# Retention and feed-forward in one kernel: the second chunk's recurrence in halves of 64 tokens, its scores and state sums issued apart

## The chip, the cores and the metric

The kernel runs on one core of a Trainium2 chip. A core has five engines that run side by side, each through its own list of instructions: TensorE (PE in the profile, with its weight loads as PEld), VectorE (DVE), ScalarE (ACT), GpSimd (POOL) and SyncE (SP, which here issues the transfers). They wait for each other by semaphores. The metric is the time of the whole program on the device, in microseconds, from repeated runs. All arithmetic is in fp32.

## The reference

Two layers follow each other. The first is a retention layer: for every batch (4) and head (8) a state of 64x64 is carried over 768 tokens. The second is a feed-forward layer of width 2048 with a leaky ReLU on 3072 rows of 512.

```
for t in range(S):                       # S = 768, D = 64
    state = gamma * state + outer(k[t], v[t])
    y[t]  = scale * (q[t] @ state)
x = y, heads side by side                # 3072 x 512
h = x @ w_in                             # 512 x 2048
out = max(0.01 * h, h) @ w_out           # 2048 x 512
```

`gamma` differs by head. Over a block of tokens the recurrence is the same as three products: the scores `k q`, masked to earlier tokens and multiplied with the block's values; a read of the state as it stood before the block; and the block's sum of `k v`, which is added to the state. The decay is put into `v` beforehand and into the result afterwards.

## The kernel before, in words

The tokens go in six chunks of 128 (`C`), each with all four batches. For each chunk the recurrence makes the layer's input `x`, and the feed-forward layer is worked in four units `u` of 512 hidden columns: `hidden` makes `g`, `output` makes `o` from it. Both use a scheme of seven products instead of eight, M1 to M7 (`seven`, product on line 662), which needs differences of blocks of `x` and `g` (`differences`, lines 606 and 609) and sums of weight blocks (`add_sums`, `last_sum`). The very first unit of chunk 0 is done plainly, in four steps for each half of the batches (`direct`, line 683).

The weights arrive as 64-bit words in pieces. ScalarE makes each piece's powers (`next_powers`, lines 578 to 583) and VectorE its mantissas (`next_mantissas`, lines 590, 595 and 602). A piece's raw words have three places, so the load of a later piece starts when VectorE has read an earlier one.

The order of the work is written out by hand: the engines execute the statements in the order in which the program issues them. Around the change this is the list of statements from line 957 on. In the names, `(1, b)` is chunk 1, batch `b`.

Before the change chunks 0 and 1 do the recurrence over all 128 tokens of a chunk at once. `score` (line 191) makes the scores of one batch, `masked` (line 211) multiplies with the mask on VectorE, `reads` (line 226) reads the state, `last_values` (261) and `first_values` (250) multiply scores and values, `state` (276) makes the sum for the state, `tokens_taken` (306) brings the result into `x`, and `state_taken` (312) adds the sum to the state. A pair of batches is done together by `products_together`. Batch 1's scores use two single banks of the dense products' pool (`score_apart`).

Chunks 2 to 5 use another form, by halves of 64 tokens and by pairs of batches. `scores_of_pair` makes scores (line 369) and both halves' state sums (line 380), masks (387), and makes the state at the middle and at the end of the chunk by two additions. `joint_visit` then multiplies the values (444), reads the state of each half (427) and takes the results (466), batch 1 before batch 0. In chunk 2 this goes into PSUM tiles of two banks, tag `att`, of which there are two places that are given out in turn: scores, sums, first and second results.

`JOINED` says from which chunk on the inputs are laid out for the second form: `q` and `k` per batch as before, but keys of a pair together and values of a pair together.

Of the kernel before, what the change touches and what calls it, by code (L numbers as in the profile page):

```python
# [22 lines left out]
def kernel(  # L23
# [113 lines left out]

    def early_inputs(c, b, kind, k):
        def do():
            place = place_of_unit(k, f"in{c}{b}_{kind}")  # L140
            flat = place.rearrange("p i k n -> p (i k n)")
            half = 2 * HP * C
            heads[c, b + kind] = [flat[:, 0:half].rearrange("p (s a t) -> p s a t", s=2, a=HP)]
            load_qk(c, b + kind)
            of_pair(c, b, kind, flat[:, half : 2 * half].rearrange(
                "p (n h d) -> p n h d", n=2, h=H))
            rooms[kind] = flat[:, 2 * half : 2 * half + 2 * HP * D]
        return do

    def spare(kind):  # L150
        return lambda: rooms[kind].rearrange("p (n a d) -> p n a d", n=2, a=HP)
# [68 lines left out]
    def reads(c, b):  # L220
        x = heads[c, b][0]
        if (c, b) not in sums_at:
            sums_at[c, b] = apart(two_banks(f"yp_{c}_{b}"))
        ps = sums_at[c, b]
        for j, m, i, a in pairs:
            mm = nc.tensor.matmul(ps[j][ts(i, 64), m, :], lhsT=st[b][ts(j, 64), a, :],
                                  rhs=x[ts(j, 64), 0, a, :], start=(m == 0), stop=False,
                                  skip_group_check=True)

        reads_done[c, b] = nc.gpsimd.memset(between, 0.0).ins  # L230
        tc.add_manual_dep(reads_done[c, b], mm.ins.name, IN_ORDER, reason="rows of the array")

    reads_done = {}
# [9 lines left out]
    def first_values(c, b):  # L243

        y, am, ps = heads[c, b][1], scores[c, b], sums_at[c, b]
        for m in range(HP // 2):
            for i in range(2):
                for j in range(2):
                    s, a = i ^ j, 2 * m + i
                    mm = nc.tensor.matmul(ps[j][ts(i, 64), m, 0:64],  # L250
                                          lhsT=y[ts(s, 64), 1, 2 * a + j, :],
                                          rhs=am[ts(s, 64), j, m, 0], start=False, stop=True,
                                          skip_group_check=True)
                    if (c, b) in reads_done:
                        tc.add_manual_dep(mm.ins, reads_done.pop((c, b)).name, IN_ORDER,
                                          reason="rows of the array")
# [73 lines left out]
    def score_apart(c, b):  # L330

        banks = [ffs.tile([128, HP * C], FP32, tag="ff", bufs=4, name=f"ap{j}_{c}_{b}")[:, 0:NS]
                 for j in range(2)]
        scores[c, b] = [ps.rearrange("p (m n t) -> p m n t", n=3, t=C // 2) for ps in banks]
        scores_to(heads[c, b][0], scores[c, b])

    def masked_apart(c, b, j):
        if j == 0:
            weights_of[c, b] = new_am(c, b)
        nc.vector.tensor_tensor(  # L340
            out=weights_of[c, b][:, j].rearrange("p m n t -> p m (n t)"),
            in0=scores[c, b][j].rearrange("p m n t -> p m (n t)"),
            in1=mask.rearrange("p n t -> p (n t)").unsqueeze(1)
                .to_broadcast([128, HP // 2, 3 * C // 2]), op=ALU.mult)
        if j == 1:
            scores[c, b] = weights_of.pop((c, b))

    weights_of = {}

# [6 lines left out]
    def scores_of_pair(c, b, banks=None, mid=None):  # L356

        if b == 0 and c > JOINED:
            next_gq()
        banks = banks or bank  # L360
        at = [banks[j].rearrange("p (b m i t) -> p b m i t", b=2, m=HP // 2, i=2)
              for j in range(2)]
        sums = [banks[2 + h].rearrange("p (b a d) -> p b a d", b=2, a=HP) for h in range(2)]
        for n in range(2):
            x = heads[c, b + n][0]
            for m, i, a in quads:
                for h in range(2):
                    for j in range(2):
                        nc.tensor.matmul(at[j][ts(h, 64), n, m, i],  # L369
                                         lhsT=x[ts(j, 64), 1, a, ts(h, 64)],  # L370
                                         rhs=x[ts(j, 64), 0, a, ts(h, 64)],
                                         start=(n == 0 and a == 0), stop=True,
                                         skip_group_check=True)
        last = c == NC - 1
        for n in range(2):
            key, val = keys.pop((c, b + n)), vals[c, b + n]
            for a in range(HP):
                for j in range(2):
                    for h in range(1 if last else 2):
                        nc.tensor.matmul(sums[h][ts(j, 64), n, a], lhsT=key[ts(h, 64), 2 * a + j],  # L380
                                         rhs=val[ts(h, 64), 2 * a + j],
                                         start=(n == 0 and a == 0), stop=True,
                                         skip_group_check=True)
        weights = scores[c, b] = []
        for j in range(2):
            am = work.tile([128, 2, HP // 2, 2, C // 2], FP32, tag=f"am{j}", name=f"am{j}_{c}_{b}")
            nc.vector.tensor_tensor(
                out=am.rearrange("p b m i t -> p (b m i) t"),
                in0=at[j].rearrange("p b m i t -> p (b m i) t"),
                in1=mask[:, 0].unsqueeze(1).to_broadcast([128, 2 * HP, C // 2]), op=ALU.mult)  # L390
            weights.append(am)
# [11 lines left out]
        if following(c, b) is not None and c > JOINED:  # L403
            of_pair(*following(c, b), 0)
# [7 lines left out]
    def joint_visit(c, b, banks=None):  # L412

        later = following(c, b) if c > JOINED else None
# [66 lines left out]
    def early_scores(c, b, place):  # L481
        def do():
            banks = [pair_of_banks(f"{name}_{c}_{b}") for name in ("ap", "sp")]
            scores_of_pair(c, b, banks[0] + banks[1], place())
        return do

    def early_visit(c, b):
        def do():
            joint_visit(c, b, [pair_of_banks(f"yp{n}_{c}_{b}") for n in range(2)])
        return do  # L490
# [366 lines left out]
    load(1, 0, unit_tile(LATE[2], "in10"))  # L857
    load(1, 1, unit_tile(LATE[1], "in11"))
# [60 lines left out]
    load(1, 2, unit_tile(LATE[0], "in12"))  # L919
# [15 lines left out]
    load(1, 3)  # L935
# [8 lines left out]
    def scored_later(b):  # L944
        score(1, b)
        masked(1, b)

    def products_together(b):
        for i in range(2):
            reads(1, b + i)  # L950
        for i in range(2):
            last_values(1, b + i)
            state(1, b + i)
        for i in range(2):
            first_values(1, b + i)

# [5 lines left out]
    scored_later(0)  # L962
    decay_v(1, 1, nc.scalar)
    next(steps)
    score_apart(1, 1)
    next_powers()
    next_mantissas()
    for j in range(2):
        masked_apart(1, 1, j)
    next_powers()  # L970
    products_together(0)
    next_mantissas()
    decay_v(1, 2, nc.scalar)
# [60 lines left out]
    def place_of_unit(k, name):  # L1034
        return work.tile([128, 7, 2, 256], FP32, tag=f"late{k}", name=name)
# [36 lines left out]
    def next_heads():  # L1072
# [15 lines left out]
        (1, 3): dict(s0=[begin_x(2), early_scores(2, 2, spare(1))],  # L1088
# [10 lines left out]
        (0, 3): dict(s0=[begin_units, early_scores(2, 0, spare(0))],  # L1099
# [159 lines left out]
    scores_of_pair(3, 0)  # L1259
# [17 lines left out]
    for n in range(N2):  # L1277
# [22 lines left out]
        if c + 1 < NC and u < 2 and following(c + 1, 2 * u):  # L1300
            scores_of_pair(*following(c + 1, 2 * u))
# [20 lines left out]
JOINED = 2  # L1322
# [87 lines left out]
```

## Time and profile before

| what | value |
|---|---|
| median of 3 runs | 638.65 us (638.64 to 639.24) |
| span of the profiled run | 637.2 us |
| TensorE busy | 630.4 us |
| VectorE busy | 462.3 us |
| ScalarE busy | 269.0 us |
| first small product of chunk 1 on TensorE | at 27.58 us |
| dense step after chunk 1's last product | at 44.63 us |
| granted TensorE clock | 1.000 |

The page gives for each engine the time in which it was busy and its share of the span. A timeline line gives the start in microseconds, the length from the first start to the last end, the engine, the line of the kernel, the tile written and those read, the shape and the count (on TensorE an fp32 product counts as two instructions). What stands in brackets at its end is idle time before it and what ended it. Lengths of neighbours overlap, because instructions are pipelined; the distance from start to start is what a group costs. In a line of busy time by stretches come: the stretch, its length, then busy time and count of PE, PEld, DVE, ACT and POOL, the granted clock, the share of the DMA engines and GB/s.

### The profile page before, as it was taken

How to read it: one execution, taken by the hardware profiler on the slowest of the kernel's cores; microseconds unless marked ns; L12 is line 12 of the kernel's file. 1: busy time of each engine (PE TensorE's matmuls, PEld its weight loads, DVE VectorE, ACT ScalarE, POOL GpSimd, SP SyncE). 2: the span in 40 equal slices, each digit the busy share in tenths (PEclk: the TensorE clock that was granted, in tenths of full speed). 3: DMA queues.
4: the chain of work that ended last, by engine and by line, in shares of the span. 5: the costliest groups of instructions: out<-in, count | busy, mean ns of one | idle time of the engine just before them, and what ended most of it. 6: DMA issues, size and time to landing. Idle time of an engine off the chain costs nothing.

```text
span 637.2 us, 14289 instructions
## 1 busy us (share of the span) xinstructions
PE 630.4 (99%) x6086; PEld 569.1 (89%) x6086; DVE 462.3 (73%) x760; ACT 269.0 (42%) x515; POOL 22.6 (4%) x45
## 2 busy tenths in 40 slices
PE   8999999999999999999999999999999999999997
PEld 5888888888888889899999999999999999999996
DVE  5679769889979976576786666877737768636655
ACT  5876556347343124242352342424333423534421
POOL 2000000000011010101000101000010000000000
PEclk9999999999999999999999999999999999999999
DMA  8931426455863999366735392864455336454301
GB/s 334 405 125 38 127 67 227 141 181 188 287 245 119 341 307 306 103 236 198 253 87 192 111 298 79 268 195 136 137 175 178 89 123 195 153 164 156 87 0 67
DMA packets 87536, 113.42 MB, mean 178 GB/s; under 512 B 3240, under 2 KB 71720, under 8 KB 87472
## 3 DMA queue, kind: packets, MB, share of 16 engines
q1 hardware_dynamic: 87168, 111.88, 53.1%
q8 instruction: 48, 0.79, 0.5%
q10 hardware_dynamic: 304, 0.62, 0.3%
q14 instruction: 16, 0.13, 0.1%
HBM read 93.35 MB, written 19.14 MB: 177 GB/s over the span
## 4 chain that ended last, share of the span: by engine, by line
PE 95%; DVE 2%; ACT 1%; DMA 1%; issue 0%; DVEq 0%; ACTq 0%
PE bank L662 32%; PE bank L1181 27%; PE C_h L662 4%; PE B_o L662 4%; PE A_h L662 4%; PE C_o L662 4%; PE A_o L662 4%; PE B_h L662 4%; PE D_h L662 2%; PE D_o L662 2%; PE d L683 2%; PE bank L369 1%; PE bank L444 1%; PE bank L427 1%; PE bank L380 1%; DMA t<-decay_dram 1%
## 5 line engine op out<-in xcount | busy, mean ns | idle before, releaser
L606 DVE TENSOR_TENSOR made<-made,bank 128x512 f32<-128x512 f32 (+1 forms) x96 | 56.3, 618 | 57.0 <-PE bank L1181 52.8
L606 DVE TENSOR_TENSOR o<-o,bank 128x512 f32<-128x512 f32 (+2 forms) x91 | 58.6, 662 | 53.4 <-PE bank L662 32.8
L662 PE MATMUL bank<-g,w 128*128 128x256 f32 x384 | 89.9, 382 | 0.0
L662 PEld LDWEIGHTS bank<-g,w 128*128 128x128 f32 x384 | 70.7, 190 | 9.2
L1181 PEld LDWEIGHTS bank<-x,wb 128*128 128x128 f32 x672 | 77.6, 192 | 0.8
L1181 PE MATMUL bank<-x,wb 128*128 128x128 f32 x672 | 77.6, 275 | 0.0
L1181 PE MATMUL bank<-x,wa 128*128 128x128 f32 x512 | 68.7, 276 | 0.1
L662 PE MATMUL bank<-gd,w 128*128 128x256 f32 x288 | 66.1, 379 | 0.0
L1181 PEld LDWEIGHTS bank<-x,wa 128*128 128x128 f32 x512 | 63.8, 192 | 1.9 <-ACT bank L1185 0.8
L662 PEld LDWEIGHTS bank<-gd,w 128*128 128x128 f32 x288 | 54.7, 190 | 7.4
L1181 PE MATMUL bank<-t,wa 128*128 128x128 f32 x384 | 53.3, 275 | 0.0
L1223 ACT ACTIVATE g<-g 128x512 f32<-128x512 f32 x64 | 39.3, 631 | 30.8 <-DVE g L606 30.8
L1181 PEld LDWEIGHTS bank<-t,wa 128*128 128x128 f32 x384 | 48.0, 192 | 0.0
L1185 ACT COPY bank<-bank 128x512 f32<-128x512 f32 (+1 forms) x32 | 16.7, 522 | 67.8 <-PE bank L1181 67.5
L606 DVE TENSOR_TENSOR g<-made 128x512 f32<-128x512 f32 x64 | 42.7, 689 | 1.2
L755 ACT COPY bank<-bank 128x512 f32<-128x512 f32 x17 | 9.7, 570 | 71.2 <-PE bank L662 71.1
L609 DVE TENSOR_TENSOR gd<-g,gd 128x512 f32<-128x512 f32 x48 | 33.2, 692 | 5.4 <-ACT g L1223 0.5
L773 ACT COPY bank<-bank 128x512 f32<-128x512 f32 x16 | 9.1, 570 | 46.4 <-PE bank L662 46.4
L662 PE MATMUL bank<-g,last 128*128 128x256 f32 x120 | 28.3, 380 | 0.0
L662 PE MATMUL bank<-gd,last 128*128 128x256 f32 (+1 forms) x124 | 27.5, 373 | 0.0
L662 PE MATMUL A_h<-x,w 128*128 128x256 f32 x112 | 26.6, 380 | 0.0
L662 PEld LDWEIGHTS bank<-gd,last 128*128 128x128 f32 x124 | 22.8, 190 | 3.2 <-DVE gd L609 0.3
(223 smaller groups left out, 1028.2 us busy)
## 6 DMA issues: line engine op xcount, KB each, us to landing
wa<-kept SPq DMA_DIRECT2D x16, 1344.0 KB, 7.2
raw<-in_weights_dram SPq DMA_DIRECT2D x31, 512.0 KB, 4.4
wb<-kept SPq DMA_DIRECT2D x16, 896.0 KB, 5.7
wa<-kept SPq DMA_DIRECT2D x16, 448.0 KB, 4.5
wb<-kept SPq DMA_DIRECT2D x16, 448.0 KB, 6.3
out_dram<-o SPq DMA_DIRECT2D x23, 256.0 KB, 2.9
kept<-w SPq DMA_DIRECT2D x12, 448.0 KB, 5.9
qk<-in_qk_dram SPq DMA_DIRECT2D x10, 512.0 KB, 8.5
```

Source lines behind the costliest of these rows:

```text
L369: nc.tensor.matmul(at[j][ts(h, 64), n, m, i], lhsT=x[ts(j, 64), 1, a, ts(h, 64)], rhs=x[ts(j, 64), 0, a, ts(h, 64)], start=(n == 0 and a = ...
L380: nc.tensor.matmul(sums[h][ts(j, 64), n, a], lhsT=key[ts(h, 64), 2 * a + j], rhs=val[ts(h, 64), 2 * a + j], start=(n == 0 and a == 0), sto ...
L427: mm = nc.tensor.matmul(at[n][j][ts(i, 64), m, ts(h, 64)], lhsT=by_half[h][ts(j, 64), n, a], rhs=x[ts(j, 64), 0, a, ts(h, 64)], start=(n = ...
L606: nc.vector.tensor_tensor(out=out, in0=a, in1=b, op=ALU.add)
L609: nc.vector.tensor_tensor(out=out, in0=a, in1=b, op=ALU.subtract)
L662: nc.tensor.matmul(to, lhsT=block(w, sa)[:, k, ts(i, 128)], rhs=rhs[:, k, a:z], start=(first and (i == 0 or split) and n == 0 and k == 0), ...
L683: nc.tensor.matmul(banks[r][:, i, :], lhsT=block(2 * u, r + 2 * kh)[:, k, ts(i, 128)], rhs=x[:, 2 * kh + th, k, :], start=(step == 0 and i ...
L755: nc.scalar.copy(out=bank_of("B"), in_=ps)
L773: nc.scalar.copy(out=bank_of("D"), in_=ps)
L1181: nc.tensor.matmul(ps[q][:, i], lhsT=w[:, j, i], rhs=part_of(moving[i], s), start=(i == 0 and m in ("M1", "M5", "M4")), stop=True, skip_gr ...
L1185: nc.scalar.copy(out=ps[3], in_=ps[0])
L1223: nc.scalar.activation(g[:, i], g[:, i], AF.Prelu, alpha=0.01)
```

## The change

Chunk 1 goes over to the form of chunks 2 to 5: pairs of batches, halves of 64 tokens. It is meant to take work from TensorE, and to need fewer small groups. In it the two parts of `scores_of_pair` are separated by a `yield`: scores and masks first, state sums and additions in a second step, with one dense step of the feed-forward layer between them. For the later chunks both steps still run one after the other. `early_visit` asks for the tile of the pair's second batch first. The inputs of chunk 1 are loaded by pairs (`inputs_into`). The functions that only the old form used go away (`reads`, `score_apart`, `masked_apart`, `scored_later`, `products_together`).

The core of the diff:

```diff
 def scores_of_pair(c, b, banks=None, mid=None):
...
+        weights = scores[c, b] = []
+        for j in range(2):
+            am = work.tile([128, 2, HP // 2, 2, C // 2], FP32, tag=f"am{j}", name=f"am{j}_{c}_{b}")
+            nc.vector.tensor_tensor(
...
+            weights.append(am)
+        yield
         last = c == NC - 1
         for n in range(2):
             key, val = keys.pop((c, b + n)), vals[c, b + n]
...
-        weights = scores[c, b] = []
-        for j in range(2):
...
-    def early_scores(c, b, place):
+    def early_scores(c, b, place, apart=False):
         def do():
             banks = [pair_of_banks(f"{name}_{c}_{b}") for name in ("ap", "sp")]
-            scores_of_pair(c, b, banks[0] + banks[1], place())
+            steps = scores_of_pair(c, b, banks[0] + banks[1], place())
+            next(steps)
+            if apart:
+                return steps
+            next(steps, None)
         return do
 
     def early_visit(c, b):
         def do():
-            joint_visit(c, b, [pair_of_banks(f"yp{n}_{c}_{b}") for n in range(2)])
+            banks = [pair_of_banks(f"yp{n}_{c}_{b}") for n in (1, 0)]
+            joint_visit(c, b, banks[::-1])
         return do
...
-    load(1, 0, unit_tile(LATE[2], "in10"))
-    load(1, 1, unit_tile(LATE[1], "in11"))
+    inputs_into(unit_tile(LATE[2], "in11"), 1, 0, 1)
+    inputs_into(unit_tile(LATE[1], "in10"), 1, 0, 0)
...
     steps = direct(0, 0, x, parts[0][1], 1)
     next(steps)
-    scored_later(0)
     decay_v(1, 1, nc.scalar)
+    sums_apart = early_scores(1, 0, spare(1, 0, 0), apart=True)()
+    next_powers()
     next(steps)
-    score_apart(1, 1)
-    next_powers()
-    next_mantissas()
-    for j in range(2):
-        masked_apart(1, 1, j)
-    next_powers()
-    products_together(0)
+    next(sums_apart, None)
+    next(steps)
+    early_visit(1, 0)()
     next_mantissas()
     decay_v(1, 2, nc.scalar)
+    decay_v(1, 3, nc.scalar)
     next_powers()
-    decay_v(1, 3, nc.scalar)
-    taken(1, 0, x1)
-    taken(1, 1, x1)
-    next(steps)
-    scored_later(2)
-    scored_later(3)
+    sums_apart = early_scores(1, 2, spare(1, 2, 1), apart=True)()
+    next_mantissas()
     later = hidden(1, 0, x1, t1, *parts[1][1:], order=FIRST)
     next(later)
     last_sum(0)
+    next_powers()
+    next(sums_apart, None)
+    early_visit(1, 2)()
     next_mantissas()
-    products_together(2)
     next_powers()
     run(steps, {})
-    tokens_taken(1, 2, x1)
-    tokens_taken(1, 3, x1)
     differences(x1, t1)
     next_gq()
-    state_taken(1, 2, for_state(sums_at[1, 2]))
-    state_taken(1, 3, for_state(sums_at[1, 3]))
     run(later, {0: [next_mantissas], 1: [lambda: differences(*parts[0][1:])],
                 2: [next_powers], 3: [lambda: add_sums(1)]})
...
-JOINED = 2
+JOINED = 1
```

More of the change, by code (lines that the diff above doesn't have):

```diff
@@ L136, in of_pair, with inputs_into, spare @@
         nc.sync.dma_start(out=place, in_=kv[c, b + kind])
+    def inputs_into(place, c, b, kind):
+        flat = place.rearrange("p i k n -> p (i k n)")
+        half = 2 * HP * C
+        heads[c, b + kind] = [flat[:, 0:half].rearrange("p (s a t) -> p s a t", s=2, a=HP)]
+        load_qk(c, b + kind)
+        of_pair(c, b, kind, flat[:, half : 2 * half].rearrange("p (n h d) -> p n h d", n=2, h=H))
+        rooms[c, b, kind] = flat[:, 2 * half : 2 * half + 2 * HP * D]
     def early_inputs(c, b, kind, k):
         def do():
[L140 to L147, printed above, removed]
-        return do
-    def spare(kind):
-        return lambda: rooms[kind].rearrange("p (n a d) -> p n a d", n=2, a=HP)
+            inputs_into(place_of_unit(k, f"in{c}{b}_{kind}"), c, b, kind)
+        return do
+    def spare(c, b, kind):
+        return lambda: rooms[c, b, kind].rearrange("p (n a d) -> p n a d", n=2, a=HP)
     def load(c, b, place=None):
@@ L218 @@
     pairs = [(j, m, i, 2 * m + i) for m in range(HP // 2) for j in range(2) for i in range(2)]
[L220 to L233, printed above, removed]
     IN_ORDER = mybir.DependencyInfo(mybir.DependencyClass.Sync, mybir.DependencyReason.DATA)
@@ L249, in first_values @@
                     s, a = i ^ j, 2 * m + i
[L250 to L256, printed above, removed]
+                    nc.tensor.matmul(ps[j][ts(i, 64), m, 0:64],
+                                     lhsT=y[ts(s, 64), 1, 2 * a + j, :],
+                                     rhs=am[ts(s, 64), j, m, 0], start=False, stop=True,
+                                     skip_group_check=True)
     def last_values(c, b):
@@ L328 @@
     room = {}
[L330 to L348, printed above, removed]
     halves_of_states = [const.tile([128, 2, HP, D], FP32, name="more_states")]
@@ L356, in scores_of_pair @@
     def scores_of_pair(c, b, banks=None, mid=None):
-        if b == 0 and c > JOINED:
+        if b == 0 and c > 2:
             next_gq()
@@ L373, in scores_of_pair @@
                                          skip_group_check=True)
+        weights = scores[c, b] = []
+        for j in range(2):
+            am = work.tile([128, 2, HP // 2, 2, C // 2], FP32, tag=f"am{j}", name=f"am{j}_{c}_{b}")
+            nc.vector.tensor_tensor(
+                out=am.rearrange("p b m i t -> p (b m i) t"),
+                in0=at[j].rearrange("p b m i t -> p (b m i) t"),
+                in1=mask[:, 0].unsqueeze(1).to_broadcast([128, 2 * HP, C // 2]), op=ALU.mult)
+            weights.append(am)
+        yield
         last = c == NC - 1
@@ L383, in scores_of_pair @@
                                          skip_group_check=True)
-        weights = scores[c, b] = []
-        for j in range(2):
[L386 to L391, printed above, removed]
         p = b // 2
@@ L402, in scores_of_pair @@
         mid_of[p] = old, mid
-        if following(c, b) is not None and c > JOINED:
+        if following(c, b) is not None and c > 2:
             of_pair(*following(c, b), 0)
@@ L412, in joint_visit @@
     def joint_visit(c, b, banks=None):
-        later = following(c, b) if c > JOINED else None
+        later = following(c, b) if c > 2 else None
         banks = banks or [[bank[k] for k in at] for at in ((1, 2), (0, 7))]
@@ L918 @@
     decay_v(0, 2, nc.scalar)
-    load(1, 2, unit_tile(LATE[0], "in12"))
+    inputs_into(unit_tile(LATE[0], "in13"), 1, 2, 1)
     masked(0, 2)
@@ L934 @@
     next_mantissas()
-    load(1, 3)
+    heads[1, 2] = [work.tile([128, 2, HP, C], FP32, tag="qk", bufs=AHEAD, name="qk_1_2")]
+    load_qk(1, 2)
+    of_pair(1, 2, 0)
     values(0, 3)
@@ L942 @@
     add_sums(0, last=False)
[L944 to L955, printed above, removed]
     xs[1] = new_x(1)
@@ L1087 @@
                      s5=[sum_of_unit(3, 0)], s6=[sum_of_unit(3, 1), early_decays(2, 2)]),
-        (1, 3): dict(s0=[begin_x(2), early_scores(2, 2, spare(1))],
+        (1, 3): dict(s0=[begin_x(2), early_scores(2, 2, spare(2, 2, 1))],
                      s1=[sum_of_unit(3, 2)], s2=[sum_of_unit(3, 3)],
@@ L1098 @@
         (1, 2): dict(s0=[sum_of_unit(2, 3)], s1=[keep_unit(2)]),
-        (0, 3): dict(s0=[begin_units, early_scores(2, 0, spare(0))],
+        (0, 3): dict(s0=[begin_units, early_scores(2, 0, spare(2, 2, 0))],
                      s1=[lambda: differences(*parts[1][1:])],
@@ L1258 @@
     halves_of_states.append(work.tile([128, 2, HP, D], FP32, tag="m5", name="half_states"))
-    scores_of_pair(3, 0)
+    products(scores_of_pair(3, 0), 2)
     for b in range(2):
@@ L1300 @@
         if c + 1 < NC and u < 2 and following(c + 1, 2 * u):
-            scores_of_pair(*following(c + 1, 2 * u))
+            products(scores_of_pair(*following(c + 1, 2 * u)), 2)
         if visiting:
```

## The prediction

> **What bounds the kernel now.** I read the page from the top: shares first, then the chain that ended last.
>
> ```profile
> span 637.2 us, 14289 instructions
> PE 630.4 (99%) x6086; PEld 569.1 (89%) x6086; DVE 462.3 (73%) x760; ACT 269.0 (42%) x515; POOL 22.6 (4%) x45
> PE 95%; DVE 2%; ACT 1%; DMA 1%; issue 0%; DVEq 0%; ACTq 0%
> ```
>
> TensorE (PE) is busy 99% of the span and is 95% of the chain. So a microsecond taken off PE in any stage is a microsecond off the end, and a microsecond for which PE waits is one added. The question is only what happens between the first small product of chunk 1 and the return to dense work. That stage is 27.58 to 44.63 us; by stretches (time, PE, weight loads, VectorE, ScalarE, ...):
>
> ```profile
> 27.50:44.60 17.10, 16.82 (x410) 14.17 (x409) 11.91 (x21) 13.84 (x38) 0.39 (x4) 1.00 0.59 215
> 44.60:56.80 12.20, 12.20 (x64) 10.75 (x57) 11.75 (x20) 6.40 (x13) 0.00 (x0) 1.00 0.17 51
> ```
>
> The reader is to see two things. PE has almost no hole in the stage, although VectorE (DVE) works for 11.91 of 17.10 us there. And in the next 12.2 us VectorE is busy 11.75: it has no room to catch up. Work pushed out of the first stretch arrives late in the second.
>
> How PE spends the stage now, from the timeline (start, length, engine, line, what, count):
>
> ```profile
> 27.58 0.90 PE L191 MATMUL ap<-in 64*64 64x128 f32 x32
> 28.41 1.99 PE L683 MATMUL d<-x,w 128*128 128x256 f32 x8
> 30.33 0.90 PE L191 MATMUL ap<-in 64*64 64x128 f32 x32
> ...
> 35.40 1.99 PE L683 MATMUL d<-x,w 128*128 128x256 f32 x8
> 37.32 0.90 PE L191 MATMUL ap<-in 64*64 64x128 f32 x32
> ...
> 38.82 1.99 PE L662 MATMUL A_h<-x,w 128*128 128x256 f32 x8
> 40.65 0.38 PE L695 MATMUL B_h<-mask 128*128 128x512 bf16 x1
> ...
> 44.63 1.99 PE L683 MATMUL d<-x,w 128*128 128x256 f32 x8
> ```
>
> Each pair of batches has a dense group between its scores and its products: VectorE's masks run behind it. At 35.40 a dense group also stands between the first pair's products and the second pair's scores; VectorE takes the first pair's results (from 35.52) behind that one.
>
> What the new form costs can be read off chunk 2, which already uses it:
>
> ```profile
> 191.88 1.16 PE L369 MATMUL ap<-in 64*64 64x64 f32 x64
> 192.86 1.11 PE L380 MATMUL sp<-in,in 64*64 64x64 f32 x64
> 193.90 1.99 PE L662 MATMUL C_h<-t,w 128*128 128x256 f32 x8
> 201.01 0.46 PE L444 MATMUL yp<-am,in 64*64 64x64 f32 x16
> 203.17 1.99 PE L662 MATMUL C_h<-x,w 128*128 128x256 f32 x8
> ```
>
> Scores and sums take 2.02 us together, a visit 2.16 us. But there 7.1 us of dense work lie between sums and visit.
>
> [...] VectorE's instructions start in program order throughout. [...] A dense group with small tiles on both sides takes 1.92 us here (28.41 to 30.33) against 1.73 us among dense ones, so I use the former. [...] the masks of 128x512 take 0.68 us each here[...].
>
> **The change, part by part.** PE, from the unchanged 27.58 us, start to start:
>
> - scores of pair 0: 1.04 (the small group before a dense one, as 192.86 to 193.90), to 28.62;
> - dense group 1.92, to 30.54; sums 1.04, to 31.58; dense group 1.92, to 33.50;
> - visit 2.10 (2.16 less the switch, since small tiles follow), to 35.60;
> - scores of pair 1: 1.04; group M1 into A_h 1.83 (38.82 to 40.65); fill 0.31 (40.65 to 40.96); sums 0.98; visit 2.16, to 41.92.
>
> Without waits the dense group of 44.63 would begin at 41.92: 2.71 us saved. This is the part the change removes: whole-token value products, wider reads, and about 0.8 us of small waits.
>
> Data is no limit. The decayed values of batch 1 are ready at 29.62 (ScalarE, unchanged), before sums at 30.54. The first pair's inputs come by the same four transfers in the same order; only which half lies in each differs. ScalarE then decays batches 2 and 3 in one run: 29.62, 1.9 for one piece's powers, 4.0 for 16 decays, to 35.5; sums of pair 1 come after that.
>
> Now the waits it adds, which the line order decides. Banks alternate between two places. In the new order, VectorE's queue after the first visit is: four takes, a weight piece's mantissas (three operations), two masks, another piece's mantissas, `last_sum`, the two additions of state sums, four takes, a third piece, then the differences.
>
> First wait: the scores of pair 1 go into the banks from which batch 1's results are taken, and no dense group lies between. In the visit batch 1 is complete about 2.07 us after its start (203.00 plus 0.07 from the end of its last product to a VectorE start, as 44.47 to 44.54), so takes begin at 35.57. Two takes are done 0.75 us later. PE waits from 35.60 to 36.37: 0.77 us. If one bank sufficed it would be 0.4.
>
> Second wait: `read(0)` of the second visit writes the banks that hold the state sums, so it waits for both additions. VectorE from 35.57: takes 1.33 (its cadence at 207.66 to 208.99), mantissas 1.9 (33.66 to 35.52), masks 1.20 (195.26 to 196.46), mantissas 1.9, `last_sum` 0.60 (40.04 to 40.64), additions 1.40 (196.46 to the end of the second at 197.86). The sum is 8.33, to 43.90, and PE goes on at 44.00. PE itself, with the first wait, is at `read(0)` at 36.37+1.04+1.83+0.31+0.98+0.28 = 40.81. It waits 3.19 us. Queued behind it on PE is everything, the dense group that needs nothing from VectorE included. If only the first addition were needed, the wait would be 2.5. The masks, done at 40.0, cost nothing: M1, fill and sums hide them.
>
> The remaining 1.88 us of the visit end at 45.88: the dense group is 1.25 us later than before.
>
> Third wait: C_h needs the first difference. Before, the differences came at once after the takes. Now a piece's mantissas stand between. Takes from 45.79, 1.33, mantissas 1.9, a difference 0.69: 49.71. PE would start C_h at 45.88+1.84+1.72 = 49.44. 0.3 us lost.
>
> Fourth: VectorE is then about 2.5 us later than before (the 0.7 us of separate state additions at 48.52 is gone, the 1.9 is added), PE 1.6 us. The copy into B_o at 58.88 has 0.8 us to spare before PE's 60.28, and it stands behind three ScalarE operations that wait for VectorE. 0 to 0.4 us; I take 0.2. After 61 us VectorE idles (2.16 us at 74.42), and the delay is absorbed.
>
> Everything later is the same work in the same order, with the state buffers' names changed. The earlier mask instruction in the text of the other chunks changes no engine's order. Sum: -2.71+0.77+3.19+0.31+0.2 = +1.76 us: 640.4.
>
> **Rivals.**
>
> - *The waits just eat the saving.* If banks free earlier (one take, one addition), first and second waits shrink by 0.4 and 0.7, and the last two vanish: 638.65-2.71+0.4+2.5+0.1 = about 638.9. For it: the estimates of readiness are to a tenth. Against it: both places are allotted as two-bank tiles.
> - *The saving comes through.* If VectorE's queue were not the limit: 638.65-2.71+0.8 = 636.7. For it: VectorE has 5 us idle in the stage now, and chunk 2 shows no such wait. Against it: the queue adds up to 8.3 us where PE has 5.2 us of work, and its idle time falls before 35.5, where it cannot be used.
> - *The delay spreads.* The pieces' raw loads start as their mantissas end, 5 to 6 us later than now. If the converted weights then miss the first output groups, another 1 to 2 us: about 642. Against it: page and stretch show under a fifth of the DMA engines busy from 44.6 to 56.8.
>
> **How the numbers follow.** Forecast 0.60, waits eating the saving 0.22, saving through 0.11, spreading 0.07. A change of 0.2% is 1.28 us, so slower begins at 639.93. Some 0.07 of the forecast falls under that. Slower 0.53+0.07 = 0.60; same 0.22+0.07 = 0.29; faster 0.11. The range reaches from the second case, 638.6, to between forecast and spreading, 641.6.
>
> **What would show it.** Right: PE idle ahead of the reads of the second visit (from about 40.8 to 44.0), released by VectorE's addition; about 0.8 us ahead of the second pair's scores, released by a take; the dense group of 44.63 at about 45.9. Wrong: that group at 42 to 43, or the additions done before PE has finished the sums. I would be wrong if VectorE's queue ran shorter than 5.5 us there, or if the reads did not wait for the banks.

## The result, and the profile after

| | before | changed |
|---|---|---|
| median of 4 runs | 638.71 us (638.64 to 639.24) | 641.51 us (640.94 to 642.57) |
| ratio, 95% interval | | 1.0044 (1.0029 to 1.0059) |
| span of the profiled run | 637.2 us | 640.7 us |

The change makes the kernel 2.8 us slower. The forecast was +1.76 us, to 640.4, with a range up to 641.6. So direction and range held, and the size was a third short. The profiled run is the slowest of the four (642.57 us), and the only one whose mean granted clock was not 1.000 but 0.997; its span is 3.5 us longer than before. In the first experiment below one run of 21 took 812.09 us at a mean clock of 0.753, and no ratio counts it.

The names below: a *visit* is what `joint_visit` does for a pair, a *take* one of the four instructions by which VectorE brings a visit's result into `x`, a *piece* a weight piece, whose mantissas are three VectorE instructions. The page of the changed kernel, shares first, then the chain that ended last:

```profile
span 640.7 us, 14552 instructions
PE 630.2 (98%) x6214; PEld 568.9 (89%) x6214; DVE 463.2 (72%) x763; ACT 269.0 (42%) x515; POOL 23.0 (4%) x45
PE 95%; DVE 3%; DMA 1%; issue 1%; ACT 0%; DVEq 0%; ACTq 0%
```

TensorE is as busy as before over the whole, but the span is longer. The chain has one per cent more of VectorE and one of "issue", which stood at 0 before. By stretches, with the same columns as before:

```profile
27.50:47.20 19.70, 15.38 (x538) 13.13 (x535) 11.24 (x22) 13.58 (x37) 0.40 (x4) 0.97 0.48 169
47.20:60.00 12.80, 12.80 (x55) 11.09 (x56) 12.25 (x22) 6.42 (x13) 0.00 (x0) 0.91 0.27 83
```

TensorE now has 4.3 us of holes in the stage, where it had 0.3. The third number from the end is the granted clock, and it is no longer 1.00. TensorE's timeline names the holes (start, length, engine, line, what, count; in brackets the idle time ahead and what ended it):

```profile
27.32 1.16 PE L334 MATMUL ap<-in 64*64 64x64 f32 x64
28.41 1.99 PE L654 MATMUL d<-x,w 128*128 128x256 f32 x8
30.33 1.24 PE L354 MATMUL sp<-in,in 64*64 64x64 f32 x64
31.50 1.99 PE L654 MATMUL d<-x,w 128*128 128x256 f32 x8
33.43 0.46 PE L410 MATMUL yp<-am,in 64*64 64x64 f32 x16
...
34.41 0.41 PE L393 MATMUL yp<-in,states 64*64 64x64 f32 x14
35.49 0.27 PE L393 MATMUL yp<-in,states 64*64 64x64 f32 x1 [0.67 <-issue]
...
37.25 0.69 PE L334 MATMUL ap<-qk 64*64 64x64 f32 x32 [0.73 <-PE yp L410]
...
41.47 0.41 PE L410 MATMUL yp<-am,in 64*64 64x64 f32 x16
44.79 0.46 PE L393 MATMUL yp<-qk,states 64*64 64x64 f32 x16 [2.92 <-DVE states L577]
...
47.02 3.16 PE L654 MATMUL d<-x,w 128*128 128x256 f32 x8
50.02 1.89 PE L633 MATMUL A_h<-x,w 128*128 128x256 f32 x8
51.74 1.89 PE L633 MATMUL C_h<-t,w 128*128 128x256 f32 x8
```

The reader is to see four things. The forecast's first wait is there, 0.73 us ahead of the second pair's scores. Its releaser is put down to TensorE itself, but VectorE's takes stand there. The second wait is there, 2.92 us ahead of the second visit's reads, ended by VectorE's state addition. A hole of 0.67 us, which nobody forecast, lies within the first visit: it ends by "issue", that is, by nothing that the profile shows. And the dense group at 47.02, 3.00 us from start to start, takes 1.16 us longer than the same group elsewhere. The clock by microseconds says why:

```profile
46.00:47.00 1.00, 1.00 (x46) 0.90 (x35) 0.27 (x1) 0.00 (x0) 0.00 (x0) 0.50 0.07 16
47.00:48.00 1.00, 1.00 (x6) 0.84 (x3) 1.00 (x4) 0.00 (x0) 0.00 (x0) 0.50 0.00 0
48.00:49.00 1.00, 1.00 (x4) 0.78 (x3) 0.97 (x3) 0.00 (x0) 0.00 (x0) 0.50 0.00 0
49.00:50.00 1.00, 1.00 (x5) 0.85 (x4) 0.90 (x3) 0.60 (x1) 0.00 (x0) 0.79 0.00 0
```

From 46.00 us, a good microsecond after its long wait had ended, TensorE ran at half clock for 3.4 us. VectorE's queue shows what the long wait is made of:

```profile
36.39 1.42 DVE L432 TENSOR_TENSOR x<-yp,dec 128x256 f32<-128x256 f32 x4 [3.37 <-PE yp L410]
37.73 0.42 DVE L561 TENSOR_SCALAR w<-raw 128x512 uint32<-128x512 uint32 x1
...
39.59 1.28 DVE L342 TENSOR_TENSOR am<-ap,mask 128x512 f32<-128x512 f32 x2
40.78 0.42 DVE L561 TENSOR_SCALAR w<-raw 128x512 uint32<-128x512 uint32 x1
...
42.64 0.68 DVE L580 TENSOR_TENSOR w<-w 128x512 f32<-128x512 f32 x1
43.24 0.68 DVE L577 TENSOR_TENSOR in<-states,sp 128x512 f32<-128x512 f32 x1
43.96 0.69 DVE L577 TENSOR_TENSOR states<-in,sp 128x512 f32<-128x512 f32 x1
```

From the first take at 36.39 to the end of the second addition at 44.65 VectorE works without a hole, 8.26 us (forecast: 8.33). It starts them in the order of the program, as all its 763 instructions in this trace, and all 760 in that of the kernel before. Just ahead of that it idled 3.37 us.

The next two lines are from before, the third is from the changed kernel, whose C_h stands above:

```profile
48.19 1.89 PE L662 MATMUL C_h<-t,w 128*128 128x256 f32 x8
56.83 1.89 PE L662 MATMUL A_o<-g,w 128*128 128x256 f32 x8
60.38 1.89 PE L633 MATMUL A_o<-g,w 128*128 128x256 f32 x8
```

C_h starts at 51.74, 3.55 us later than before (48.19); A_o starts 3.55 later too (60.38 against 56.83), and the span is 3.5 longer. So in this run all of the loss arises in this stage, and nothing after 52 us adds to it or gives it back.

### The profile page after: what moved, and what is told of

Read it like the earlier page. It is cut to its first block, busy times and chain, and to the rows that moved or that the text cites. A ratio compares the mean times of both kernels' runs of the same rounds, so it can differ in the third digit from the quotient of the medians.

```text
span 640.7 us, 14552 instructions
## 1 busy us (share of the span) xinstructions
PE 630.2 (98%) x6214; PEld 568.9 (89%) x6214; DVE 463.2 (72%) x763; ACT 269.0 (42%) x515; POOL 23.0 (4%) x45
## 4 chain that ended last, share of the span: by engine, by line
PE 95%; DVE 3%; DMA 1%; issue 1%; ACT 0%; DVEq 0%; ACTq 0%
PE bank L633 32%; PE bank L1133 27%; PE C_h L633 4%; PE B_o L633 4%; PE A_o L633 4%; PE C_o L633 4%; PE B_h L633 4%; PE A_h L633 4%; PE d L654 3%; PE D_o L633 2%; PE D_h L633 2%; PE bank L334 1%; PE bank L410 1%; PE bank L393 1%; PE bank L354 1%; DMA t<-decay_dram 1%
```

## The experiments

The theory to be tested: the loss is the second wait, and it is set by what stands ahead of the state additions in VectorE's queue. Two rivals came out of the profile: the half clock, and the hole of "issue". Each kernel below is the changed kernel with the edit shown. Each ran beside the kernel before, whose medians were 638.81 to 639.47 us.

**One piece's mantissas out of the queue, into VectorE's idle time.**

```diff
     next(sums_apart, None)
+    next_mantissas()
     next(steps)
     early_visit(1, 0)()
-    next_mantissas()
```

> The first weight piece's mantissas are moved ahead of the first visit, into VectorE's idle time at 33 to 36 us; nothing else changes. Theory (VectorE's queue ahead of the state additions sets the second wait): the masks then follow the takes as soon as the scores are there, the additions end at about 43.5 instead of 44.7, the wait ahead of the second visit's reads falls from 3.0 to about 1.8 us, the time from 641.5 to about 640.2. Rival (the wait is the latency from the last sum over the additions to the bank, whatever stands before them in the queue): the wait stays at 3 us and the time at 641.5.

Median 639.93, ratio to before 1.0013 (1.0006 to 1.0019): 1.6 us of the 2.8 are back. The wait:

```profile
43.39 0.64 PE L393 MATMUL yp<-qk,states 64*64 64x64 f32 x16 [1.80 <-DVE states L577]
```

1.80 instead of 2.92 us. VectorE's queue sets this wait.

**One piece more ahead of the additions.**

```diff
     next_powers()
+    next_mantissas()
     next(sums_apart, None)
     early_visit(1, 2)()
-    next_mantissas()
     next_powers()
```

> The third piece's mantissas are put ahead of the second pair's state additions instead of behind the second visit: the suspected wait is made longer by one piece, 1.9 us, with the same work in all. Theory of the queue: the wait ahead of the reads grows from 3.0 to 4.9 us; the differences come 1.9 us sooner behind the visit, so C_h can't wait; time +1.6 to +1.9 us, about 643.3. Rival of latency: no change, 641.5. If a long idle time lowers TensorE's clock, a stretch at half clock of about 3 us follows more often than behind 3.0 us of waiting, and costs another 1.6 us in such runs.

Median 644.97, ratio 1.0094 (1.0080 to 1.0108), more than the expected 643.3. The reads start 1.69 us later than in the changed kernel (46.48 against 44.79), as the theory has it; the wait itself grew by 2.25, because TensorE also came to it earlier. But the time grew by 3.5. The first line is the wait, the others are stretches around it:

```profile
46.48 0.71 PE L393 MATMUL yp<-qk,states 64*64 64x64 f32 x16 [5.17 <-DVE states L577]
```

```profile
44.00:46.00 2.00, 0.00 (x0) 0.00 (x0) 1.64 (x3) 0.42 (x1) 0.00 (x0) 0.71 0.64 164
46.00:48.00 2.00, 1.52 (x56) 1.55 (x60) 0.34 (x1) 0.00 (x0) 0.00 (x0) 0.50 0.43 168
48.00:50.00 2.00, 2.00 (x68) 1.88 (x62) 0.61 (x2) 0.00 (x0) 0.10 (x1) 0.50 0.03 8
50.00:52.00 2.00, 2.00 (x6) 1.61 (x6) 1.93 (x5) 0.21 (x1) 0.00 (x0) 0.59 0.00 0
```

The clock falls at 44.83, still within the wait, and is back at 51.66. So after 5.17 us of idling TensorE works at half clock for 5.2 us. Whether that is what costs the rest, the next kernel tests.

**The same long queue, with TensorE kept busy in the wait.** To the edit above, 22 dense products are added in `joint_visit`, ahead of the second visit's reads; nobody reads what they write.

```diff
+        for _ in range(22 if (c, b) == (1, 2) else 0):
+            fill_bank(at[1][0])
```

> The kernel with the longer wait (third piece ahead of the additions), but PE spends the wait on 22 dense products of 512 columns, about 4.8 us, which write a bank that the visit's first group then overwrites; they are extra work and change no result. Theory of the clock (a wait of 5 us drops TensorE to half clock for about 6 us, and that is what took 644.97 instead of 643.3): the granted clock stays at 1.0 through the stage, time about 643.2. Rival (the clock falls for another reason, or the loss is in the wait itself): half clock again, 645.0 or more.

Median 642.83, ratio 1.0060 (1.0047 to 1.0073). The reads start when they did in the kernel above, at 46.55 against 46.48, and the clock stays:

```profile
46.55 0.46 PE L393 MATMUL yp<-qk,states 64*64 64x64 f32 x16 [0.18 <-DVE states L579]
```

```profile
46.00:48.00 2.00, 1.82 (x113) 1.71 (x117) 0.40 (x1) 0.00 (x0) 0.20 (x2) 1.00 0.45 168
48.00:50.00 2.00, 2.00 (x37) 1.75 (x28) 1.72 (x5) 0.49 (x1) 0.00 (x0) 1.00 0.00 0
```

With the same delay at full clock the kernel takes 2.1 us less. So the clock's fall is a price of its own, paid after the wait, and work without any use takes it away.

**The dense group between the second pair's sums and its visit.** It needs nothing from the state, and was queued behind the wait.

```diff
     next(sums_apart, None)
+    run(steps, {})
     early_visit(1, 2)()
     next_mantissas()
     next_powers()
-    run(steps, {})
```

> The dense step behind the second visit is moved between its sums and the visit, where the first pair has one; VectorE's order stays. Theory of the queue: the wait ahead of the reads falls by the step's 1.9 us to about 1.1, but now only one group stands between visit and C_h, and VectorE's takes, mantissas and first difference need 4 us: C_h waits about 2 us. Net within 0.4 us of the changed kernel, 641.5. Rival (the lack of a dense step there is the cause, not VectorE's queue): the 1.9 us are gained, 639.6.

Median 640.86, ratio 1.0035 (1.0023 to 1.0048), 0.65 us below the changed kernel. The wait was moved more than removed:

```profile
44.72 0.46 PE L393 MATMUL yp<-qk,states 64*64 64x64 f32 x16 [0.83 <-DVE states L577]
...
50.43 1.75 PE L633 MATMUL C_h<-t,w 128*128 128x256 f32 x7 [1.93 <-DVE t L580]
```

With the dense group gone from behind the visit, C_h waits for the differences. They stand in the same queue behind the takes and a third piece's mantissas.

**Both, and the third piece behind the additions.**

```diff
     next(sums_apart, None)
+    next_mantissas()
     next(steps)
     early_visit(1, 0)()
-    next_mantissas()
...
     next(sums_apart, None)
-    early_visit(1, 2)()
     next_mantissas()
-    next_powers()
     run(steps, {})
+    early_visit(1, 2)()
+    next_powers()
```

> Both moves, and the third piece's mantissas directly behind the state additions, where VectorE would wait for the visit. Theory of the queue: no wait ahead of the reads (below 0.3 us), C_h waits about 0.4 us behind the visit; C_h starts at about 47.5 against 48.2 in the kernel before, time 638.0, faster than both kernels. Rival (something else in the new form is slow): it stays above 639.5.

Median 638.02, ratio 0.9989 (0.9983 to 0.9996): 3.5 us faster than the changed kernel, and 0.9 us faster than the kernel before. VectorE's work is the same, and so are TensorE's products; only the order differs. The reads wait for nothing now:

```profile
42.95 0.46 PE L410 MATMUL yp<-am,in 64*64 64x64 f32 x16
43.23 0.41 PE L393 MATMUL yp<-qk,states 64*64 64x64 f32 x16
...
47.18 1.97 PE L633 MATMUL C_h<-t,w 128*128 128x256 f32 x8 [0.20 <-DVE t L580]
```

This version is faster than both kernels, though by only 0.11% against the kernel before. With the two experiments on one piece it shows that the order of VectorE's queue and of the dense group is the main cause.

**The old order of asking for the visit's tiles.**

```diff
-            banks = [pair_of_banks(f"yp{n}_{c}_{b}") for n in (1, 0)]
-            joint_visit(c, b, banks[::-1])
+            joint_visit(c, b, [pair_of_banks(f"yp{n}_{c}_{b}") for n in range(2)])
```

> The tiles of a visit are asked for in the old order again (first batch's first), also in chunk 2; nothing else is undone. Theory (the two places are given out in turn, and a wait is set by who wrote in that place before): the second pair's scores then wait for all four takes instead of two, 0.7 us more, and the whole second visit waits for the additions instead of all but its first group, 0.3 us more: about 642.5. Rival (the order is of no account): 641.5.

Median 641.95, ratio 1.0048 (1.0037 to 1.0060). Both waits are what they were, 0.73 and 2.91 us. The longer waits that the theory expected did not come: the order of asking is of no account for these waits, and the forecast's reason, that banks alternate between two places, is not what decides which takes a wait needs. The waits derived from it are right in size all the same. What does decide it was not tried.

**The first pair's sums directly behind its scores; the dense group behind the visit.**

```diff
-    sums_apart = early_scores(1, 0, spare(1, 0, 0), apart=True)()
+    early_scores(1, 0, spare(1, 0, 0))()
     next_powers()
     next(steps)
-    next(sums_apart, None)
-    next(steps)
     early_visit(1, 0)()
+    next(steps)
```

> In the first pair the state sums follow the scores directly, and the dense step that stood between them goes behind the first visit, ahead of the second pair's scores. VectorE's order of instructions is unchanged. Theory (the first wait, 0.7 us, is there because no dense work covers the takes; the second is set by VectorE's queue): the first wait vanishes, the sums wait about 0.4 us for the decayed values, VectorE starts its takes about 1.9 us sooner and PE comes to the second visit at about the same time, so the second wait falls to 1.8 us; time about 639, near the kernel before. Rival (what counts is that scores and sums are apart): the additions come too late for the first visit, and the time is not below the changed kernel's 641.5.

Median 640.84, ratio 1.0035 (1.0023 to 1.0047), where about 639 was expected. The first wait is gone, and the second fell to 1.82 us, as expected. But the gain went into a new hole:

```profile
28.22 0.66 PE L354 MATMUL sp<-in,in 64*64 64x64 f32 x31
30.77 0.73 PE L354 MATMUL sp<-in,in 64*64 64x64 f32 x33 [1.90 <-issue]
...
44.12 0.46 PE L393 MATMUL yp<-qk,states 64*64 64x64 f32 x16 [1.82 <-DVE states L577]
```

Again "issue", here after 31 of 64. A first thought was that these sums wait for ScalarE's decays of the second batch, whose part begins there.

**All of the good moves together:** sums behind scores, the dense group behind the first visit, two pieces' mantissas early, and the second pair's end as in the fastest kernel.

```diff
-    sums_apart = early_scores(1, 0, spare(1, 0, 0), apart=True)()
+    early_scores(1, 0, spare(1, 0, 0))()
...
-    next(sums_apart, None)
-    next(steps)
-    early_visit(1, 0)()
     next_mantissas()
+    early_visit(1, 0)()
+    next(steps)
+    next_powers()
     decay_v(1, 2, nc.scalar)
     decay_v(1, 3, nc.scalar)
-    next_powers()
-    sums_apart = early_scores(1, 2, spare(1, 2, 1), apart=True)()
     next_mantissas()
+    sums_apart = early_scores(1, 2, spare(1, 2, 1), apart=True)()
...
     next(sums_apart, None)
-    early_visit(1, 2)()
     next_mantissas()
-    next_powers()
     run(steps, {})
+    early_visit(1, 2)()
+    next_powers()
```

> All together: sums directly behind the scores in the first pair with its dense step behind the visit, two pieces' mantissas in VectorE's idle time ahead of the second pair's masks, the third behind the additions, the last dense step between sums and visit of the second pair. Theory of the queue: no wait above 0.4 us between the first scores and C_h, which starts at about 46 us; time 636.8, 2 us under the kernel before, near the 2.7 us that the new form was worked out to save. Rival (new form is no cheaper on PE): not below 638.

Median 639.25, ratio 1.0007 (1.0001 to 1.0014), a miss: 636.8 was expected. All waits above 0.21 us are gone but the new hole, and in the profiled run a dense group at half clock follows it:

```profile
30.92 0.77 PE L354 MATMUL sp<-in,in 64*64 64x64 f32 x33 [1.93 <-issue]
31.62 3.60 PE L654 MATMUL d<-x,w 128*128 128x256 f32 x8
```

**What is this hole?** Where it comes, it comes after the same count of TensorE's product instructions, from the stage's first: 64+31 = 95 in the last two kernels, and 64+8+64+8+64+14 = 222 in the changed kernel and in the one with early mantissas, although quite different work stands there. The distance is 127. Each such instruction has its weight load, which makes 254. The pages list transfers of instructions as a queue of their own, here in the changed kernel and, second, in the kernel before:

```profile
q8 instruction: 49, 0.80, 0.5%
q8 instruction: 48, 0.79, 0.5%
```

49 packets of together 0.80 MB are 16 KB each. The changed kernel has 6214 product instructions and 6214 weight loads on TensorE, the kernel before 6086 of each: in both 254 to a packet, as many as lie between the two places. By this count, an estimate from the pages, the queue is TensorE's, a packet is a block of some 254 of its instructions, and the breaks stand where a new block begins. To test it, first 28 more TensorE instructions (14 products with their weight loads) were put at the start, in the changed kernel and in the one with the sums behind the scores:

```diff
-    keep_busy(10)
+    keep_busy(8)
+    for _ in range(16):
+        nc.tensor.matmul(idle[:, 0, 0:8], lhsT=nothing, rhs=nothing[:, 0:8], start=True, stop=True,
+                         skip_group_check=True)
```

> The changed kernel with 28 more instructions at TensorE's start (16 tiny products for two of the ten warming ones), otherwise the same. In its profile PE stops for 0.7 us inside the first visit, after 14 of 16 products of a read, with no wait in the list. Theory (PE's list of instructions is read in blocks, and the next block is late): the break moves 14 products forward, to the beginning of that group. Rival (it waits for something of the visit): it stays where it is.

> The kernel with sums directly behind the scores in the first pair, with the same 28 more instructions at TensorE's start. Its break of 1.9 us in the sums came after 31 of 64 products. Theory of the block of instructions: it comes after 17 now, about as long. Rival (the second batch's values, decayed by ScalarE until 29.4 us, are what it waits for): it stays at 31 or 32 of 64, where the second batch begins.

One run of each: 642.91 and 641.42 beside 638.81 for the kernel before. They tell little. With less work at the start the stage began 2.5 us later (29.92 and 29.85; in the first the clock was at half from 7.15 to 13.98, in the second the trace records no fall), and the break in the first visit of the one, or after 31 of the sums in the other, was no longer to be seen. That the second has none after 31 speaks against ScalarE's decays, but weakly, because everything came later. So a smaller dose was put where TensorE waits for weights anyway, ahead of 13.4 us:

```diff
     keep_busy(1)
+    for _ in range(8):
+        nc.tensor.matmul(idle[:, 0, 0:8], lhsT=nothing, rhs=nothing[:, 0:8], start=True, stop=True,
+                         skip_group_check=True)
```

> The changed kernel with eight tiny products (8 columns, bf16) in the hole ahead of 13.4 us, where TensorE waits for weights anyway, so that the stage should start at the same 27.3 us. The break in the first visit came after 64+8+64+8+64+14 = 222 products counted from the first scores. Theory of the instruction stream (the break stands at a fixed number of instructions): eight products sooner, after 214, that is after 6 of those 16 products instead of 14, 0.4 to 0.8 us long. Rival (a thing of the work itself, such as an operand or a bank of that product): after 14 as before.

> The same eight tiny products in the kernel whose first pair's sums follow its scores at once; there the break came after 31 of 64 products of the sums (95 from the first scores) and took 1.9 us. Theory of the instruction stream: after 23 of the sums, 1.9 us or somewhat more (the end of the break is set by when the instructions arrive, about 30.8 us). Rival (the sums wait for ScalarE's decays of the second batch, half of the 64): after 31 as before.

One run of each: 640.88 and 641.34 beside 639.47. The stage starts at 27.30 and 27.45. The first, which is the changed kernel with the eight:

```profile
34.31 0.30 PE L393 MATMUL yp<-in,states 64*64 64x64 f32 x6
34.87 0.38 PE L393 MATMUL yp<-in,states 64*64 64x64 f32 x9 [0.27 <-issue]
```

The break comes after 6 instead of 14, exactly eight sooner; at 0.27 us it is shorter than the expected 0.4 to 0.8. The second, with the sums behind the scores; its first line is from the view of 28.40 to 28.90 us alone:

```profile
28.43 0.54 PE L354 MATMUL sp<-in,in 64*64 64x64 f32 x23
```

```profile
28.43 1.45 PE L354 MATMUL sp<-in,in 64*64 64x64 f32 x64
...
32.72 0.41 PE L393 MATMUL yp<-in,states 64*64 64x64 f32 x14
35.12 0.27 PE L393 MATMUL yp<-in,states 64*64 64x64 f32 x1 [1.99 <-issue]
```

The first break has moved to where it was expected, after 23 of the sums: the 23rd product starts at 28.75 and the 24th at 28.96, where most of the group follow within 0.05 us. But it takes 0.2 us and not 1.9, so its length was a miss. After 31 there is none, against the rival of ScalarE's decays. A break of 1.99 us stands further on, after 64+64+8+16+16+16+16+14 = 214, again eight less than 222. So the hole belongs to the instruction stream and not to the work that stands in it: this is shown.

What sets its length can be read from the transfers of this queue in the traces. In every kernel with a break of 0.2 us or more at one of these two places, the product behind the break starts 1.26 to 1.54 us after a 16 KB transfer has ended. Seven of these eleven breaks:

| kernel | transfer ends | next product |
|---|---|---|
| sums behind scores, first break | 29.29 | 30.77 |
| all together | 29.48 | 30.92 |
| changed | 34.06 | 35.49 |
| early mantissas | 33.89 | 35.27 |
| changed, with eight more | 33.49 | 34.87 |
| sums behind scores, with eight more, both breaks | 27.69, 33.58 | 28.96, 35.12 |

So the breaks fit a wait of TensorE for its next block. In four traces of the table it shows that the sooner TensorE gets to the second place, counted from the transfer's end, the longer is the break: 1.99 us where it got there 0.45 us ahead of that end (sums behind scores, with eight more), 0.67 at 0.76 us behind it (changed), 0.40 at 0.98 (early mantissas), 0.27 at 1.11 (changed, with eight more). The changed kernel with 28 more instructions came to both boundaries 3.2 us after such a transfer, and has no break there. Why the transfers come no earlier was not tried. Once begun, those of the table take 1.0 to 1.1 us, not longer than the ones from 35 to 60 us (0.9 to 1.4). The input loads fill these engines up to about 33 us (in the changed kernel: busy share 1.03 and 408 GB/s from 28 to 32), and a block was used up in 4.2 us (127 products from 28.96 to 33.13 in the kernel with the sums behind the scores and eight more); that the block's transfer begins late because of those loads is argued only.

## Why the prediction was right, and what it lacked

Its steps against the changed kernel's profile, and against the one with eight more instructions, where the clock stayed at 1.00 (us from start to start, so that most waits are a little longer than the brackets of the timeline; the first visit goes to the end of its last product, and the first wait is the bracket behind it):

| step | forecast | changed | with eight more |
|---|---|---|---|
| scores, dense, sums, dense | 5.92 | 6.11 | 6.03 |
| first visit, break included | 2.10 | 3.09 | 2.68 |
| first wait | 0.77 | 0.73 | 0.73 |
| scores, A_h, fill, sums | 4.16 | 4.22 | 4.21 |
| first group of the second visit | 0.28 | 0.28 | 0.28 |
| second wait | 3.19 | 3.04 | 3.05 |
| rest of the visit | 1.88 | 2.23 | 1.79 |
| dense group | 1.84 | 3.00 | 1.84 |
| A_h and the wait of C_h | 2.03 | 1.72 | 2.08 |
| sum | 22.17 | 24.42 | 22.69 |

- *The saving on TensorE (2.71).* Right in the dense groups and nearly in the small ones, which cost up to 0.13 more each; a first visit without a break takes the 2.10 forecast (35.95 to 38.05 in the kernel with 28 more instructions). What the forecast calls the switch is a difference between groups in the trace of before: a dense group takes 1.92 us between small ones and 1.73 among dense ones (48.19 to 49.92), a small group 1.04 ahead of a dense one and 0.98 ahead of a small one. Of the parts named for it, the 0.8 us of small waits is not to be seen as idle time: TensorE idled 0.28 us in the stage before. Without waits it would have come through; the fastest kernel shows part of it.
- *First wait (0.77).* 0.73, right.
- *Second wait (3.19).* 3.04, right, and its cause is shown: it shrinks by 1.1 when a piece leaves the queue, grows by 2.25 when one is added (0.57 of it because TensorE comes sooner), and is gone when the dense group and the early mantissas go together. The rivals "saving comes through" and "waits just eat the saving" fall with it. The reasoning that VectorE's idle time lies before 35.5 and cannot be used held only for the order as written.
- *Third wait (0.31).* Its own figures, 49.71 and 49.44, give 0.27; the sum took 0.31. In the changed kernel's profile it is hidden by the slow dense group; with the clock at 1.00 it is 0.36 by this count.
- *Fourth (0.2).* Not there: A_o starts as late as C_h.
- *Later work the same; the delay does not spread.* Right.
- *Banks alternate.* Not the reason for these waits, without effect on the sum.

At full clock the forecast is short by 0.52 us from the first scores to C_h, where the break in the first visit alone cost 0.58 (2.68 against 2.10); the start, 0.28 us earlier than the 27.58 it took, gives back half. So the mechanism was right, and the size was short by two terms that the sum did not have. It treated a wait on TensorE as costing its own length, and it took TensorE's instructions to be always at hand. The half clock after the wait cost 0.35+1.16 = 1.5 us in the profiled run, less the 0.3 us of C_h's wait that it hid. The clock averaged 0.997 over the profiled run, and 1.000 over the other three. The half clock itself lasted 3.4 us in each of the four traces where it followed a hole of 1.80 to 2.92 us (46.00 to 49.42 in the changed kernel), and 6.83 us in the one with 5.17 (44.83 to 51.66). It does not follow every wait, and how long TensorE must idle for it was not shown: 1.80 us of waiting was followed by half clock in the profiled run of the kernel with early mantissas, and 2.91 us was not in the changed kernel with eight more. A mean clock of 0.997 by itself proves no wait: the kernel before, whose longest hole in the stage is 0.20 us, shows it once in 68 runs (640.16 us). The other term is the break in the instruction stream, 0.67 us in the timeline and 0.99 in the table.

The half clock belongs to the profiled run: the median lies between two runs at a mean clock of 1.000. What the forecast lacked there is the break, and a rest that is not placed. That the range held is in part luck. Its upper end, 641.6, stood halfway to a spread of the delay to later groups, which did not happen; the median, 641.51, is just below it for another reason, and one of the four runs lies above it.

What stays open: the three runs at full clock took 640.94 to 641.53 us, 2.2 to 2.8 above before. The forecast with a break that costs 0.58 to 0.99 us, as in the table, and with the earlier start comes to an estimated 2.1 to 2.5. Those runs left no trace, so whether their breaks were of that size isn't known, and even then some 0.3 us is not placed.

## What to carry to other kernels

Before TensorE's work is moved closer together, write down the in-order queue of the engine that has to free its banks, and put work that can wait (here a weight piece's mantissas) into that engine's idle time ahead of the critical stretch; the same instructions in another order made 3.5 us here, between the medians. Put dense work that needs nothing ahead of the wait rather than behind it, and see who was hidden behind it before. And price a TensorE wait like these at more than its length, since the clock may fall after it: it fell in some runs with waits of 1.8 to 2.9 us, and in all four runs of the kernel with 5.17.

## What the runs showed of the hardware

A wait of 5.17 us was followed by 5.2 us of work at half clock; the same span filled with products that nobody reads kept the clock at 1.00 and gained 2.1 us. Runs of small fp32 products outran their own instruction stream here: breaks of 0.2 to 1.99 us stand at a fixed count, 127 product instructions apart, move by eight products when eight are added ahead of them, and end 1.26 to 1.54 us after a 16 KB transfer of instructions.
